# Sigmoid attention with a token-mixing MLP: 64x64 tiles, output blocks per batch, named PSUM banks and a new order of steps

## The chip, the core and the metric

The kernel runs on one core of a Trainium2 chip. A core has a matrix engine (TensorE, called PE in the profile, with its weight loads as PEld), a vector engine (DVE), a scalar engine (ACT), a general engine (POOL) and a queue engine (SP) that here only issues DMAs. Matrix products are written to PSUM, which the kernel holds as 8 banks of 128 x 512 float32, used mostly in four pairs; everything else lies in SBUF. The metric is the device time of one execution in microseconds (us). Three runs of the kernel before gave 185.79, 185.96 and 186.71 us; the median is 185.96 us.

## The reference

For 8 batches of 12 heads, with 448 tokens and 64 features per head:

```python
scores = q @ k.T / 8 - log(448)              # per batch and head
x = (sigmoid(scores) @ v)                     # heads laid side by side: (8, 448, 768)
wq, wk = x @ w_q, x @ w_k                     # (8, 448, 64) each
W_tok = wq @ wk.T / 8                         # (8, 448, 448)
out = relu(W_tok @ x) @ w_out                 # (8, 448, 768), float32
```

There is no softmax, so a sigmoid block needs nothing from its neighbours. The kernel uses (wq @ wk.T) @ x = wq @ (wk.T @ x): wk.T @ x is a 64 x 768 matrix, called `tmp`, and the 448 x 448 matrix is never made.

## The kernel before, in words

**Units.** The four heads of a batch that are worked together are a quad; 8 batches give 24 quads, three per batch. Tokens of a head lie as 7 blocks of 64. For each quad and each block there is one score step (letter `S` in the plan, function `scores`): four 64x64 matmuls of 448 columns into one pair of banks, and one sigmoid on ACT over 128 x 896 that writes a tile `at`. So there are 168 score steps and 168 sigmoids. Seven value steps (`P` or `p`, `values`) accumulate the quad's product with v in a pair of banks, and a copy to SBUF makes `xt`, which is x transposed.

**q and k** come from HBM in float32. They are cast to bfloat16, most of them on POOL, and must be transposed. There are several ways, chosen by letter: on PE with a copy out of PSUM (`q`, `k`, `a`, `b`), on DVE by its 32x32 stream transpose after POOL has exchanged quadrants (`c`, `d`; `arrange`, three pairs of POOL copies per quad), or on DVE alone with four more transposes of 32 partitions (`r`, `s`, `z`; `quadrants`).

**The MLP of a batch.** `tr_x` (`x`, `X`, `y`, `Y`) transposes `xt` to `xn`, in 64x64 tiles or whole; the token axis is padded from 448 to 512. `mlp_wqk` (`W`, `L`, `l`) makes wq and wk, in whole-array matmuls or in 64x64 tiles whose two halves are added on DVE. `mlp_wkn` (`N`) transposes wk, `mlp_tmp` or `mlp_tmp_tiled` (`U`, `T`) makes `tmp`, `mlp_mix` (`M`, `m`) multiplies it with wq and applies the ReLU on DVE or ACT into `mx`. The output product (`O`, `o`, `I`, `i`) then has three forms, for pairs of batches w = 0 to 3: `out_chunk` in whole-array matmuls over 128 tokens (w = 0 and most of w = 3), `out_pair` in 64x64 tiles (w = 1 and 2, listed in `TW`) and `out_halves` (the first half of w = 3). Results are copied to `o` tiles, or late to the idle load buffers `ld`, and stored by DMA on SP, the last ones on ACT's queue.

**Order.** `PLAN` is a string written by hand; a loop reads it letter by letter and issues the work in that order, so every engine's order is fixed by it. `ORDER` gives the order of loads and casts: six load buffers form a ring, a load is issued when the buffer's last content was cast, and `BEHIND` holds five loads back until a numbered matmul has run. `F` in the plan issues a matmul of zeros, 512 columns wide, that computes nothing; ten of the eleven such matmuls of 512 columns stand before the 20th score, and 32 smaller ones run at the very start. Pairs of banks are given out first in, first out by `bank2`; `bank1` gives half a pair.

**What limits overlap.** A score step needs a free pair. Pairs are also held by value sums (seven steps long), by output blocks, by transposes and by the MLP's products. When the pair of a score was last read by the sigmoid just before it, PE and ACT take turns.

Of the kernel before, what the change touches and what calls it, by code (L numbers as in the profile page):

```python
# [17 lines left out]
def kernel(  # L18
# [49 lines left out]
    free2 = [0, 1, 2, 3]  # L68
    halves = []

    def bank2():
        n = free2.pop(0)
        return n, pairs[n], pairs16[n]

    def bank1():
        if halves:
            n, b = halves.pop(0)
        else:
            n, b = free2.pop(0), 0
            halves.append((n, 1))  # L80
        return (n, b), pairs[n][:, b], pairs16[n][:, b]

    def release(fb):
        if isinstance(fb, int):
            free2.append(fb)
        elif (fb[0], 1 - fb[1]) in halves:
            halves.remove((fb[0], 1 - fb[1]))
            free2.append(fb[0])
        else:
            halves.append(fb)  # L90
# [5 lines left out]
    spare = singles.tile([P, 8], F32)  # L96
# [3 lines left out]
    xts = [singles.tile([P, 2, 512], BF16, name=f"xt{n}") for n in range(2 * NJ)]  # L100
    wqks = [singles.tile([P, 512], BF16, name=f"wqk{n}") for n in range(2)]
    wq2s = [singles.tile([P, S], BF16, name=f"wq2{n}") for n in range(2)]
# [25 lines left out]
    def xt(u, j):  # L128
        return xts[u % 2 * NJ + j]


    TW = (1, 2,)
# [3 lines left out]
        "FSSFFFFKSSSqFFSSkFFSSDPpSFpPSPPPqSSkPSPPSSpPpPSabSXSPpSSPSPr"  # L136
        "PXpSPSSFSszSWWWWXSPWWPSppPNSpPSqkSSUSXSMSPpSMPpSppPSSqkSPpPP"
        "SPSWWcPSPXSWWSSdMWXSWSPpPpSpNPPSqSkSUSxSMSPpppSppSCPoSOSMSOo"
        "SqCkSOoCMSpPpSDpPcPSPSdoOSSocOSLLDLSXSdLLSLPPpSppPSPSoOSoSNC"
        "xSOcDSUSPPDSPprCdPpSPpSsPpPDPSPSoPSXoSMSOoSzLLxSLLLLScSoXoSM"  # L140
        "ppDpSPpDCSpdPSOOcSpppSpPSPPSONMSYOSxSOdOSpPpPpSSDPPoOSxSUcSL"
        "LLDdSSLLLppPSppPPSoSoMSOcSOSDdPpPPSPMoPSoPmOSOScdOoSxoSDOSON"
        "oSxSOOSSUpSppPSMcpPpLLLSLpPSPdLLpDDPPSOpoSxoSOmocDSoMSodooDS"
        "NOSoSOSPPPPDtcpSppOoSMoSODoSoSdMOOSPPScpppPSOPmoOSoxoDSdOSoS"
        "OLLSLLLSLoSooNxScoPppxSpdPSPPoSODDSoSOSOOSxoSOSTppPpPSpPpPpP"
        "mPppmmWWWWWWyyINiiitiiIMiiMMIiioOoOoOOoOoOoOOOO"
    )
    PLAN = "".join(PLAN)
    KIND = ["a"] + [t for t in PLAN if t in "qacer"]
# [6 lines left out]
    def arrange(n, eng):  # L156

        arranged.add(n)
        if KIND[n] in "er":
            return  # L160
# [21 lines left out]
    def load1(n, nm, eng, m):  # L182
        u, j = quads[n]
        if KIND[n] in "cer" and nm != "v":
# [19 lines left out]
    def cast1(n, nm, e):  # L204
        if KIND[n] in "cer" and nm != "v":
# [48 lines left out]
    moves = []  # L254

    def move():
        n, m = moves.pop(0)
        for g in range(2):
            for h in range(2):
                own, other = 64 * g + 32 * h, 64 * g + 32 * (1 - h)  # L260
                nc.sync.dma_start(
                    out=qk[n][other : other + 32, h].rearrange("p t i n -> p (t i n)"), in_=m[own : own + 32, 1 - h],
                )

    def tr(n, nm, kind):
# [9 lines left out]
        if kind in "cdef":  # L275
# [5 lines left out]
            if kind in "ef":  # L281
                if t == 0:
                    moves.append((n, p_mv.tile([P, 2, 2 * S], BF16, tag="mv", name="mv")))
                nc.vector.transpose(out=moves[-1][1][:, t].bitcast(F32), in_=w)
# [5 lines left out]
        if kind in "abh":  # L290
            transposes_whole(ps[:, t], t16, slice(0, NI))
        else:
            transposes(ps[:, :, t * S : (t + 1) * S], t16, slice(0, NI))
# [9 lines left out]
        if t == 1:  # L303
            qk[n] = p_qk.tile([P, 2, 2, NI, NP], BF16, tag="qk", name="qk")
            copy = COPY["s" if kind in "jh" else "v"]
            if kind in "abh":
                copy(
                    out=qk[n].rearrange("p h t i n -> p t i h n"),
                    in_=ps[:, :, 0 : 2 * S].rearrange("p t (i h n) -> p t i h n", i=NI, h=2),
                )  # L310
            else:
                copy(
                    out=qk[n].rearrange("p h t i n -> p t h (i n)"),
                    in_=ps[:, :, 0 : 2 * S].rearrange("p h (t x) -> p t h x", t=2),
                )
# [19 lines left out]
    def values(n, i, tail, eng):  # L335
# [10 lines left out]
        if i == NI - 1:  # L346
            if tail:
                for h in range(2):
                    COPY["vs"[h]](out=xt(u, j)[:, h, 0:S], in_=ps[:, h, 0:S])  # L349
            else:  # L350
                COPY[eng](out=xt(u, j)[:, :, 0:S], in_=ps[:, :, 0:S])  # L351
# [4 lines left out]
    def tr_x(n, tail, whole, eng):  # L356
        u, j = quads[n]
        if j == 0:
            xns[u] = p_x.tile([P, 4, D], BF16, tag="xn", name="xn")
        if whole:  # L360
            fb, _, ps = bank1()
            ps = ps.rearrange("p (m g h d) -> p m g h d", m=4, g=2, h=2)
            for h in range(2):
                for m in range(4):
                    mt(
                        ps[:, m, :, h], xt(u, j)[:, h, m * P : (m + 1) * P], ident16
                    )
# [603 lines left out]
```

## Time and profile before

| what | value |
|---|---|
| median of three runs | 185.96 us |
| profiled execution, first to last instruction | 184.0 us |
| PE busy | 174.7 us (95%) |
| ACT busy | 162.7 us (88%) |
| DVE busy | 133.1 us (72%) |
| POOL busy | 124.3 us (68%) |
| moved by DMA | 48.51 MB, mean 264 GB/s |

The profiled execution's span is 184.0 us; the time of a run counts some 2 us more than that span (185.96 - 184.0 = 1.96 us against the median). Busy time on PE includes matmuls that wait in its pipeline, so a busy PE need not run at its peak; four 64x64 matmuls run side by side in the array, so their durations overlap. Rows of groups give the number of instructions, the union of their busy time, and the mean duration of one. Rows of the timeline give start, length, engine, line, operation and count of a merged group, with the idle time before it in brackets.

### The profile page before, as it was taken

The numbers are of one execution on the slowest core, as the hardware profiler recorded it, in microseconds if no ns is written. First come the engines' busy times: TensorE is split into PE (matmuls) and PEld (weight loads), VectorE is DVE, ScalarE is ACT, GpSimd is POOL, SyncE is SP. The second block draws the span as 40 slices with busy tenths as digits, with TensorE's granted clock in tenths as the row PEclk, the third lists the DMA queues.
The fourth block names the chain that finished last, engine by engine and source line by source line (L and its number), as shares of the span: only waits on it lengthen the run. The fifth ranks groups of instructions, "written<-read, shape, count | busy, mean of one in ns | idle before, by whom it ended". The sixth has DMA issues, their size and how long they took to land.

```text
span 184.0 us, 8547 instructions
## 1 busy us (share of the span) xinstructions
PE 174.7 (95%) x3662; PEld 115.3 (63%) x3662; DVE 133.1 (72%) x209; ACT 162.7 (88%) x209; POOL 124.3 (68%) x171
## 2 busy tenths in 40 slices
PE   7888989999999999999999999999999999999990
PEld 7344545554545464565555778667898878869660
DVE  3334878788798887899797788587678476686820
ACT  4699999999999999999999989999999989876230
POOL 1458799995799899779999996999999920000000
PEclk9999999999999999999999999999999999999998
DMA  5999999969999999989987984798997443422596
GB/s 177 356 385 383 328 361 360 379 229 304 331 357 326 298 289 332 344 291 315 337 298 232 349 284 145 221 321 226 352 309 226 106 125 89 116 62 60 133 237 171
DMA packets 26085, 48.51 MB, mean 264 GB/s; under 512 B 3968, under 2 KB 19968, under 8 KB 26048
## 3 DMA queue, kind: packets, MB, share of 16 engines
q1 hardware_dynamic: 25888, 47.79, 79.9%
q8 instruction: 28, 0.46, 1.1%
q10 hardware_dynamic: 160, 0.20, 0.4%
q14 instruction: 9, 0.07, 0.1%
HBM read 35.78 MB, written 11.01 MB: 254 GB/s over the span
## 4 chain that ended last, share of the span: by engine, by line
PE 78%; ACT 14%; issue 3%; DVE 2%; ACTq 0%
PE banks L119 73%; ACT at L329 13%; PE banks L122 6%; DVE xt L351 1%; DVE mx L480 1%; ACTq L661 0%; DVE ld L680 0%; DVE wqk L426 0%; ACT xt L349 0%; ACT wq L428 0%; ACT ld L678 0%; DVE zeros L716 0%; ACTq L329 0%; ACTq L678 0%; ACTq L428 0%
## 5 line engine op out<-in xcount | busy, mean ns | idle before, releaser
L329 ACT ACTIVATE at<-banks 128x896 bf16<-128x896 f32 x168 | 141.2, 932 | 4.8 <-PE banks L119 4.3
L119 PE MATMUL banks<-wout,mx 64*64 64x384 bf16 (+2 forms) x954 | 68.5, 323 | 0.0
L119 PE MATMUL banks<-qk 64*64 64x448 bf16 x672 | 61.8, 358 | 2.0 <-ACT at L329 1.3
L119 PEld LDWEIGHTS <-mx 64*64 64x64 bf16 (+1 forms) x954 | 41.1, 105 | 14.4 <-issue 5.1
L119 PE MATMUL banks<-at,v 64*64 64x448 bf16 x672 | 45.6, 351 | 0.2
L119 PEld LDWEIGHTS <-qk 64*64 64x64 bf16 x672 | 25.5, 105 | 21.4 <-issue 12.6
L209 POOL CAST qk<-ld 128x896 bf16<-128x896 f32 x28 | 33.6, 1210 | 5.4 <-DVE qk L280 1.4
L119 PEld LDWEIGHTS <-v 64*64 64x64 bf16 x672 | 22.7, 106 | 9.2 <-issue 2.4
L351 DVE CAST xt<-banks 128x896 bf16<-128x896 f32 x19 | 20.7, 1088 | 10.2 <-PE banks L119 9.8
L480 DVE TENSOR_SCALAR mx<-banks 128x1024 bf16<-128x1024 f32 (+2 forms) x21 | 21.1, 1011 | 3.9 <-PE banks L119 3.1
L219 POOL CAST v<-ld 128x896 bf16<-128x896 f32 x23 | 21.6, 954 | 1.9 <-DMA ld<-in_v_dram 1.6
L168 POOL COPY qk<-qk 32x448 uint32<-32x448 uint32 x28 | 16.4, 587 | 1.6
L280 DVE STREAM_TRANSPOSE qk<-qk 128x448 f32<-128x448 f32 x28 | 17.4, 629 | 0.0
L171 POOL COPY qk<-swap 32x448 uint32<-32x448 uint32 x28 | 15.9, 568 | 1.6
L165 POOL COPY swap<-qk 32x448 uint32<-32x448 uint32 x28 | 15.7, 562 | 1.7
L560 DVE COPY o<-banks 128x768 f32<-128x768 f32 x11 | 10.5, 952 | 5.7 <-PE banks L119 4.1
L122 PEld LDWEIGHTS <-xt 64*64 64x64 bf16 (+1 forms) x528 | 10.9, 107 | 3.6 <-issue 2.4
L119 PE MATMUL banks<-xt,wqk 64*64 64x448 bf16 (+1 forms) x138 | 12.7, 350 | 0.1
L122 PE MATMUL banks<-ident,xt 64*64 64x64 bf16 (+1 forms) x528 | 12.4, 198 | 0.1
L395 DVE COPY xn<-banks 128x1024 bf16<-128x1024 bf16 (+1 forms) x14 | 9.0, 648 | 3.3 <-PE banks L122 2.7
L119 PE MATMUL banks<-wqk,tmp 64*64 64x256 bf16 (+1 forms) x72 | 8.9, 298 | 0.1
L119 PE MATMUL banks<-wq,tmp 64*64 64x256 bf16 (+1 forms) x72 | 9.0, 300 | 0.0
(73 smaller groups left out, 159.1 us busy)
## 6 DMA issues: line engine op xcount, KB each, us to landing
ld<-in_q_dram SPq DMA_DIRECT2D x24, 448.0 KB, 5.8
ld<-in_v_dram SPq DMA_DIRECT2D x24, 448.0 KB, 5.7
ld<-in_k_dram SPq DMA_DIRECT2D x23, 448.0 KB, 6.2
out_dram<-o SPq DMA_DIRECT2D x42, 192.0 KB, 4.8
ld<-in_moe_w_out_dram SPq DMA_DIRECT2D x6, 384.0 KB, 6.2
out_dram<-ld SPq DMA_DIRECT2D x11, 192.0 KB, 2.8
wout<-wout SPq DMA_DIRECT2D x12, 96.0 KB, 6.7
out_dram<-ld SPq DMA_DIRECT2D x4, 96.0 KB, 2.4
```

Source lines behind the costliest of these rows:

```text
L119: products.append(nc.tensor.matmul(*args, **kw))
L122: products.append(nc.tensor.transpose(*args, **kw))
L165: eng.tensor_copy(out=z[lo], in_=w[hi, 0])
L168: eng.tensor_copy(out=w[hi, 0], in_=w[lo, 1])
L171: eng.tensor_copy(out=w[lo, 1], in_=z[lo])
L209: COPY[e](out=f[:, :, "qk".index(nm)].rearrange("p e i d y -> p e y i d"), in_=ld.pop((nm, n)).rearrange("p (y i e d) -> p e y i d", y=2, ...
L219: COPY[e](out=t16.rearrange("p i b d -> p b i d"), in_=ld.pop((nm, n)).rearrange("p b (i d) -> p b i d", i=NI),)
L280: nc.vector.transpose(out=qk[n][:, t].rearrange("p t i n -> p (t i n)").bitcast(F32), in_=w)
L329: nc.scalar.activation(at, sc[:, :, 0:S], ACTF.Sigmoid, bias=attn_bias, scale=attn_scale)
L351: COPY[eng](out=xt(u, j)[:, :, 0:S], in_=ps[:, :, 0:S])
L480: nc.vector.tensor_scalar(dst, ps, moe_scale, 0.0, ALU.mult, ALU.max)
L560: COPY["s" if act else "v"](out=o, in_=ps[:, :, 0:NB])
```

## The change

- **Token axis without padding.** `xt` is laid out as 7 blocks of two 64-wide halves, `xn` as 7 blocks of 64 per head pair. `tr_x` makes 28 tiled or 7 whole transposes per quad instead of 32 or 8. `mlp_wkn` makes 14 transposes instead of 8, `mlp_tmp` always runs in 64x64 tiles into a pair of banks (28 matmuls of 192 columns), with one copy out.
- **wk product.** `W` steps may be whole or tiled as before, by letter. In all there are 72 tiled and 30 whole matmuls (120 and 18 before).
- **Output blocks per batch.** `TW` becomes (1, 2, 3). An output block covers tokens of one batch, and one block per pair of batches joins the middle tokens of both. For that, wq is extended by 32 columns (`extended`), and `mlp_mix` uses 224 columns in place of 256. `out_halves` and the late case of `out_chunk` are gone; batches 0 and 1 keep the whole-array form.
- **Last store.** The last block is copied in two halves by DVE and ACT and stored in eight DMAs of 32 x 384, four on SP and four on ACT.
- **Banks by name.** `BANKS` lists for each step which pair (0 to 3) or bank (a to h) it takes.
- **Order.** `PLAN` and `ORDER` are new. The fillers `F`, the list `BEHIND`, casts by DVE and ACT (marked with a dot before), and memsets of the padding are gone. More quads are transposed by DVE alone (`r`): the program has 24 + 8 more stream transposes on DVE, fewer casts there, and 12 more q or k casts of that layout on POOL.

```diff
-    free2 = [0, 1, 2, 3]
-    halves = []
+    BANKS = (
+        "abcd01230130213201301301230130123123c20d32c032d0120210231021"
...
+    given = list("".join(BANKS))
+    held = set()
     def bank2():
-        n = free2.pop(0)
+        n = int(given.pop(0))
...
-    TW = (1, 2,)
+    TW = (1, 2, 3,)
     PLAN = (
-        "FSSFFFFKSSSqFFSSkFFSSDPpSFpPSPPPqSSkPSPPSSpPpPSabSXSPpSSPSPr"
...
-        "mPppmmWWWWWWyyINiiitiiIMiiMMIiioOoOoOOoOoOoOOOO"
+        "SSSKSSDqSDSkSPPSPSDSPPDqkSPPrSSSPspPSSpSSPDDpzPprSxSsPPPSSPp"
...
+        "SoSOpDPppSppSPoOSoSUPopPMmppPLPLlMLyLLxOyoONoOUOoMoOmOMOOoOO"
+        "ooOoOooOOOOOo"
     )
 def tr_x
-        for m in range(4):
-            for h in range(2):
+            for i in range(NI):
                 for g in range(2):
-                    for c in range(2):
+                    for h in range(2):
                         mt(
-                            ps[HALF[c], g, (2 * m + h) * HD : (2 * m + h + 1) * HD],
+                            ps[HALF[h], g, i * NP : (i + 1) * NP], xt(u, j)[HALF[g], h, i],
...
 def mlp_tmp
-        for m in range(4):
+        for i in range(NI):
             for y in range(2):
-                mm(
-                    ps[HALF[y]], wkn[u][:, m, :], xns[u][:, m, y * NB : (y + 1) * NB],
+                for x in range(2):
+                    mm(
+                        ps[HALF[x], y, 0 : NJ * DH], wkn[u][HALF[y], i, :], xns[u][HALF[y], NJ * x : NJ * x + NJ, i, :],
...
 def out_pair
+        at = S // 2 - 32 if len(us) == 2 else k * NP + (32 + S // 2 if us[0] else 0)
         for b in range(3 * part, 3 * part + 3):
-            for y, (u, i) in enumerate(blocks):
+            for y in range(2):
+                st = mx[HALF[y], b, at : at + NP]
...
+        def store_last():
             for y in range(2):
                 for x in range(2):
+                    cols = slice(x * NB, (x + 1) * NB)
+                    dma = (nc.scalar if y else nc.sync).dma_start
+                    for u in us:
+                        dma(
+                            out=out[2 * w + u].rearrange("(r n i) d -> i r n d", r=2, i=NI)[NI // 2, y, :, cols],
+                            in_=o[64 * x + 32 * u : 64 * x + 32 * u + 32, y],
+                        )
...
-    BEHIND = {("w", 1): 728, ("v", 8): 856, ("q", 22): 2264, ("v", 20): 2392, ("v", 23): 2648}
+    BEHIND = {}
```

More of the change, by code (lines that the diff above doesn't have):

```diff
@@ L289, in tr @@
         fb, _, ps = ps_qk[n]
[L290 to L293, printed above, removed]
+        transposes(ps[:, :, t * S : (t + 1) * S], t16, slice(0, NI))
         if n == 1:
@@ L396, in tr_x @@
+        if tail:
+            for g in range(2):
+                COPY["vs"[g]](out=xn[:, g], in_=ps[:, g])
+        else:
+            COPY[eng](out=xn, in_=ps)
         release(fb)
@@ L474, in mlp_tmp_tiled @@
+        COPY["s" if act else "v"](out=tmps[u], in_=ps[:, :, 0 : NJ * DH])
         release(fb)
@@ L556, in out_pair @@
         if part < 3:
-            opened.append((w, blocks, part + 1, fb, ps))
+            opened.append((w, us, k, part + 1, fb, ps))
             return
-        o = o_tile([P, 2, NB])
-        COPY["s" if act else "v"](out=o, in_=ps[:, :, 0:NB])
+        late = len(cast) == len(ORDER) + 2
+        last = w == NU // 2 - 1 and len(us) == 2
+        o = ld_next()[:, 0:D].rearrange("p (b x) -> p b x", b=2) if late else o_tile([P, 2, NB])
+        if last:
+            for y in range(2):
+                COPY["vs"[y]](out=o[:, y], in_=ps[:, y, 0:NB])
+        else:
+            COPY["s" if act else "v"](out=o, in_=ps[:, :, 0:NB])
         release(fb)
-        (u0, i0), (u1, i1) = blocks
         def store():
@@ L625, in out_halves @@
+        stores.append((o_tiles[0] - 1, store_last if last else store))
+        if tail or late:
             flush()
```

453 lines of the change are left out of this document (165 added, 288 removed), and 10 rows, old and new, of the table ORDER.

## The prediction, made before the changed kernel had run

> **What bounds the kernel now.** I read the page, then the busy time by stretch, then the timeline. From the page:
>
> ```profile
> span 184.0 us, 8547 instructions
> ...
> PE 174.7 (95%) x3662; PEld 115.3 (63%) x3662; DVE 133.1 (72%) x209; ACT 162.7 (88%) x209; POOL 124.3 (68%) x171
> ...
> PE 78%; ACT 14%; issue 3%; DVE 2%; ACTq 0%
> ```
>
> By the chain this is a PE kernel. Cut at the first sigmoid (6.29 us), the end of the last (160.99) and the last matmul (179.70), it looks otherwise (columns: length, then busy time of PE, PEld, DVE, ACT, POOL, granted clock, DMA share, GB/s):
>
> ```profile
> 6.29:51.00 44.71, 41.12 (x860) 21.91 (x857) 31.31 (x43) 44.31 (x54) 35.12 (x43) 1.00 0.98 342
> 51.00:98.00 47.00, 46.77 (x804) 26.34 (x803) 40.88 (x58) 46.59 (x60) 42.05 (x57) 1.00 0.95 315
> 98.00:161.00 63.00, 63.00 (x1630) 49.38 (x1632) 46.25 (x64) 59.38 (x73) 45.81 (x65) 1.00 0.72 222
> ...
> 179.70:184.00 4.30, 0.00 (x1) 0.00 (x0) 0.36 (x1) 0.32 (x1) 0.00 (x0) 0.80 0.59 164
> ```
>
> Up to 161 us ACT is busy in 44.31 + 46.59 + 59.38 = 150.3 of 154.7 us. PE only catches up from 98 us on, and there ACT still has 94%. So there are two limits almost at the same height, and whatever is taken from PE counts only until ACT is full. What a sigmoid costs ACT, with the first and the last of them:
>
> ```profile
> 6.29 1.73 ACT L329 ACTIVATE at<-banks 128x896 bf16<-128x896 f32 x2 [0.63 <-PE banks L119]
> ...
> 8.33 4.97 ACT L329 ACTIVATE at<-banks 128x896 bf16<-128x896 f32 x6 [0.32 <-PE banks L119]
> ...
> 98.65 9.97 ACT L329 ACTIVATE at<-banks 128x896 bf16<-128x896 f32 x12 [0.24 <-PE banks L119]
> ...
> 160.07 0.92 ACT L329 ACTIVATE at<-banks 128x896 bf16<-128x896 f32 x1 [0.68 <-PE banks L119]
> ```
>
> Twelve in 9.97 us is 0.831 us each, 139.6 us for the 168 of them. The phase of sigmoids runs from 6.29 to 160.99, 154.7 us.
>
> **The change part by part: ACT.** What else ACT does within that phase:
>
> ```profile
> L478 ACT ACTIVATE mx<-banks 128x1024 bf16<-128x1024 f32 x3 | 3.1, 1028 | 0.0
> ...
> L351 ACT CAST xt<-banks 128x896 bf16<-128x896 f32 x3 | 2.7, 912 | 0.0
> L560 ACT COPY o<-banks 128x768 f32<-128x768 f32 x3 | 2.4, 805 | 0.0
> ...
> L680 ACT COPY o<-banks 128x384 f32<-128x384 f32 x5 | 2.4, 482 | 0.1
> ...
> L370 ACT COPY xn<-banks 128x1024 bf16<-128x1024 bf16 x1 | 1.0, 1006 | 0.0
> ```
>
> That is 3.1 + 2.7 + 2.4 + 2.4 + 1.0, and one more copy of 128x384 (0.5): 12.1 us. With the sigmoids 151.7, which leaves 3.0 us of the 154.7 in which ACT has nothing or stretches. In the changed program ACT has, ahead of its last sigmoid, 6 copies of 128x384 (2.9), 5 ReLUs of 896 (as the sigmoid's 0.92: 4.6), one xn copy of 896 (at most 1.0) and a copy of 64x448 with one of 64x32 (not in these rows; between 0.5, one copy of 384, and 1.0, two; I take 0.7, since the second is small): 9.2 us. ACT is relieved of 2.9 us. If its idle 3.0 stays, the phase takes 139.6 + 9.2 + 3.0 = 151.8 us. One piece of that idle time is the 0.32 us ahead of the third sigmoid: the plan began with two scores and now issues three before the transposes `K`, so I drop it: 151.5 us, **3.2 less**.
>
> **PE** must keep that pace. What a matmul and a change of shape cost:
>
> ```profile
> 87.15 0.36 PE L119 MATMUL banks<-qk 64*64 64x448 bf16 x4
> 87.44 1.15 PE L119 MATMUL banks<-wout,mx 128*128 128x384 bf16 x6
> 88.52 0.38 PE L119 MATMUL banks<-qk 64*64 64x448 bf16 x4
> 88.73 0.74 PE L119 MATMUL banks<-at,v 64*64 64x448 bf16 x12
> 89.30 0.36 PE L119 MATMUL banks<-qk 64*64 64x448 bf16 x4
> ```
>
> From start to start, 12 tiled matmuls of 448 take 0.57 us: 448 columns at 2.4 per ns, a quarter for each, is 0.56. Six whole ones of 384 take 1.08, against 6 x 0.16 = 0.96; the four ahead of them 0.29 against 0.187. So tiled and whole work cost the same per column, and each passage between the two shapes loses 0.10 to 0.12 us. In the order of the programs there are 84 passages before and 51 after: 33 x 0.11 = 3.6 us less.
>
> Columns: of the x transposes
>
> ```profile
> L122 PE MATMUL banks<-ident,xt 64*64 64x64 bf16 x448 | 6.2, 194 | 0.0
> L122 PE MATMUL banks<-ident,xt 128*128 128x128 bf16 x80 | 6.2, 220 | 0.1
> ...
> L119 PE MATMUL banks<-zeros 128*128 128x512 bf16 x11 | 3.4, 381 | 0.3 <-ACT at L329 0.2
> ```
>
> (448 x 16 + 80 x 128) / 2400 = 7.25 us become (532 x 16 + 35 x 128) / 2400 = 5.41. By the same count, from the two programs, q and k transposes go from 3.73 us (336 tiled, 28 whole) to 1.76 (184 and 10; DVE takes the others), tmp from 4.88 (40 of 384 columns on half the array, 42 on a quarter) to 4.48 (224 of 192), the mix from 4.80 (96 of 256, 48 of 448) to 4.48 (144 of 224, 24 of 448), wk transposes from 0.85 (64 on half the array) to 1.49 (112), zeros beside the first 32 from 2.4 to 0. Scores, values, wk product and output blocks keep their columns (816 tiled and 126 + 12 whole output matmuls become 1008 and 84 of the same sum). Together 6.3 us fewer, and 9.9 with the passages; the stretch behind the last score grows by 0.5 (below), so 10.4 in the phase. PE sinks below ACT there, and PE's saving beyond 3.2 us buys nothing. The Trainium skill, TensorEngine Tiling (Array Packing), section Performance Considerations, "PSUM Bottleneck", warns that tiling speeds TensorE and not the evacuation of PSUM. If PE alone counted, the time would fall by over 10 us; by that rule it does not, and ACT's rows above agree.
>
> **DVE** gets more:
>
> ```profile
> L249 DVE STREAM_TRANSPOSE qk<-qk 32x448 f32<-32x448 f32 x8 | 5.1, 636 | 0.2
> ...
> L480 DVE TENSOR_SCALAR mx<-banks 128x1024 bf16<-128x1024 f32 x9 | 11.0, 1224 | 2.5 <-PE banks L119 1.8 <-ACT xt L351 0.6
> ...
> L312 DVE COPY qk<-banks 128x1792 bf16<-128x1792 bf16 x5 | 5.4, 1089 | 1.0 <-ACT at L329 0.6 <-PE banks L122 0.3
> ...
> L209 DVE CAST qk<-ld 128x896 bf16<-128x896 f32 x4 | 3.5, 883 | 0.0
> ```
>
> 32 more stream transposes by 0.636 are +20.4 us. Away go those 4 casts and 5 of k, v and wout (as 0.883: 7.9), 3 of 5 qk copies (3.3) and an eighth of nine ReLUs (1.2). The rest has both signs and I leave it: +8 us. In the phase DVE is busy 31.3 + 40.9 + 46.3 = 118.4 us and idle 36.3; it would be busy 126 of 151.5, idle 25. I cost this at nothing; its cover is that idle time, and what it costs without it is rival A.
>
> **POOL** gets 12 casts more and 12 exchange copies fewer:
>
> ```profile
> POOL 1458799995799899779999996999999920000000
> ...
> L209 POOL CAST qk<-ld 128x896 bf16<-128x896 f32 x28 | 33.6, 1210 | 5.4 <-DVE qk L280 1.4
> ...
> L165 POOL COPY swap<-qk 32x448 uint32<-32x448 uint32 x28 | 15.7, 562 | 1.7
> ```
>
> 12 x 1.21 - 12 x 0.56 = +7.8, less six plain q and k casts, plus three of v and wout (nearest row 1.21 each): +4. POOL's work ended in slice 33 of 40, each 4.6 us, so by 152; 4 more end by 156, ahead of the last sigmoids. That is its cover, and I cost it at nothing; uncovered, the last scores come up to 4 us late. Loads keep their bytes; dropping `BEHIND` only lets five of them start earlier.
>
> **Tail.** Behind the last score:
>
> ```profile
> 159.61 0.40 PE L119 MATMUL banks<-qk 64*64 64x448 bf16 x4
> ...
> 162.22 0.87 PEld L119 LDWEIGHTS <-wqk 128*128 128x128 bf16 x6 [0.36 <-issue]
> ...
> 163.46 0.62 PEld L122 LDWEIGHTS <-xt 64*64 64x64 bf16 x64 [0.37 <-issue]
> ...
> 179.34 0.58 ACTq L661 DMA_DIRECT2D out_dram<-ld  x1
> 180.04 0.32 ACT L678 COPY ld<-banks 128x192 f32<-128x192 f32 x1 [1.79 <-PE banks L119]
> 180.39 0.50 ACTq L661 DMA_DIRECT2D out_dram<-ld  x1
> ```
>
> PE goes from 159.61 to 179.70, 20.09 us. Columns behind the last score: 18.46 us (9 values 1.68, mixes 1.12, wk products 1.12, transposes 0.54, tmp 0.56, output 5.76 tiled and 7.68 whole) and three passages (0.33); 1.30 is waiting in the chain xt, wk product, wk transpose, tmp, mix. Afterwards 19.33 us (7 values 1.31, mixes 1.12, wk products 1.12, transposes 0.75, two tmp 1.12, 29 steps of output 13.92), no passage. Output steps now stand between all links of that chain, so I take 0.4 of waiting, from 0 to the old 1.3: 19.7 us, **0.4 less**. The end, from the last matmul to the last instruction, is 4.30 us. After the change each half of the last block is 128x384 (0.48 against 0.32), and four stores instead of one stand behind it on ACT's queue, and as many on SP's. An issue takes 0.50 to 0.58, so the last one comes 3 x 0.53 later: **1.8 more**, bounds 0 (if issues overlap) and 2.3 (if the last ones also wait 0.5 for earlier stores).
>
> **Sum** on the profiled span: 184.0 - 3.2 - 0.4 + 1.8 = 182.2; with the 1.96 us between span and median, **184.2 us**, 0.9% faster.
>
> **Rivals.** A, DVE takes ACT's place. With 32 more transposes in order before copies that free banks, a late copy holds a pair and the next score waits. If DVE needed all 36.3 us of idle time that it had, the phase would take 126.4 + 36.3 = 162.7 us, 11 over my 151.5; with half of that, 189.8 us, slower. It decides as soon as DVE needs more than 25 us. For it: from 51 to 98 us DVE is already busy 87%. Against: much of its idle time ends on PE, which now comes earlier.
>
> B, the cold clock eats the gain. The first matmuls ran at half speed:
>
> ```profile
> 0.98 3.60 PE L119 MATMUL banks<-zeros 128*128 128x128 bf16 x32 [0.98 <-DVE zeros L716]
> ```
>
> 112 ns per 128 columns, against 53 at 2.4 per ns. Without the fillers PE has 9.4 us of columns for the first 24 scores in 20 us. At half speed that is 18.9, still covered, but each score takes 0.19 longer; a third of 24 uncovered is 1.5: 185.7 us, no change. Against: granted clock 1.00 in the three stretches with sigmoids. The Trainium skill, TensorE: Matmul & The Clock Gate, Part 1, puts the drop behind an idle window of about 3.4 us; by that rule it does not happen here.
>
> C, ACT's idle time goes as well, since PE no longer holds it up and banks are named: another 3.0 us, 181.2. For it: scores whose pair was last read by the sigmoid right before fall from 8 to 3 in the programs.
>
> **How the numbers follow.** Forecast (183.2 to 185.0) 0.42, C (below) 0.20, B (to 186.9) 0.18, A 0.20. 0.5% is what a measurement here can tell from no change: faster 0.62, same 0.18, slower 0.20. The range goes from C, 181.0, over B to a third of A's full price, 187.8; the forecast's own is 183.2 to 185.0.
>
> **What would show it.** Last sigmoid's end near 157.8 (ACT step), the last score 1.4 ahead of it as before; ACT over 97% busy up to there; PE with gaps in 98 to 158; last matmul near 176.2; 6.1 us from it to the end; four stores in a row on ACT's queue. DVE as the releaser of scores would mean A; whole matmuls at 112 ns per 128 columns before 30 us B. If the phase isn't shorter at all, my main step is wrong.

## The result and the profile after

| kernel | runs | median us | lowest to highest |
|---|---|---|---|
| before | 4 | 186.05 | 185.79 to 186.71 |
| after | 4 | 190.78 | 190.10 to 191.81 |

The changed kernel is slower: ratio 1.026, with a 95% interval of 1.021 to 1.031, where 0.9% faster was forecast. Here and below, a median and a range are of all executions of a kernel, while a ratio and its interval leave out those that took over 1.5% longer than the fastest of the same kernel. From its page, the rows that answer those of before:

```profile
span 189.7 us, 8858 instructions
...
PE 170.4 (90%) x3835; PEld 118.2 (62%) x3835; DVE 139.9 (74%) x211; ACT 159.7 (84%) x201; POOL 125.0 (66%) x167
...
PEclk9966999999999999999999999999999999999998
...
PE 68%; DVE 16%; issue 5%; DMA 4%; ACT 3%; SPq 1%; POOL 0%; DVEq 0%; ACTq 0%
```

PE and ACT are both busy less than before, in a longer span: nobody took over, time went empty. The same cuts as before, by stretch (length, then busy time of PE, PEld, DVE, ACT, POOL, granted clock, DMA share, GB/s):

```profile
6.27:51.00 44.73, 37.50 (x783) 21.04 (x784) 35.10 (x53) 43.36 (x53) 36.29 (x43) 0.92 0.96 332
51.00:98.00 47.00, 44.91 (x806) 25.49 (x802) 42.31 (x63) 44.26 (x58) 39.31 (x51) 1.00 0.95 311
98.00:165.10 67.10, 64.48 (x1650) 51.79 (x1653) 49.55 (x69) 61.03 (x72) 48.04 (x67) 1.00 0.70 217
...
184.25:189.70 5.45, 0.01 (x3) 0.00 (x0) 0.56 (x1) 0.48 (x1) 0.00 (x0) 0.84 0.59 153
```

The phase of sigmoids now runs from 6.27 to 165.07, 158.8 us instead of 154.7. What ACT has to do in it (groups of that stretch):

```profile
L308 ACT ACTIVATE at<-banks 128x896 bf16<-128x896 f32 x168 | 141.4, 928 | 10.2 <-PE banks L122 7.9 <-issue 1.1
L441 ACT ACTIVATE mx<-banks 128x896 bf16<-128x896 f32 x5 | 4.6, 917 | 0.2 <-PE banks L122 0.2
L587 ACT COPY o<-banks 128x384 f32<-128x384 f32 x6 | 3.0, 498 | 0.0
L360 ACT COPY xn<-banks 128x896 bf16<-128x896 bf16 x1 | 0.9, 912 | 0.0
L407 ACT CAST wq<-banks 64x448 bf16<-64x448 f32 x1 | 0.5, 524 | 0.3 <-DVE wqk L403 0.3
L409 ACT CAST wq<-banks 64x32 bf16<-64x32 f32 x1 | 0.2, 176 | 0.0
```

Its work beside the sigmoids is 4.6 + 3.0 + 0.9 + 0.5 + 0.2 = 9.2 us, as forecast. With the 139.6 of the sigmoids that makes 148.8, and 10.0 us of the 158.8 are left as idle time, where the forecast had 2.7. Nearly all of that stands ahead of sigmoids, and PE ends it. So the question is what holds PE up.

**Place one: 98 to 125 us.** PE's timeline of the changed kernel, the rows around three of its gaps (the bracket is the idle time ahead of a row and what ended it; "issue" means that PE waited for nothing that the profile shows):

```profile
112.48 0.35 PE L122 MATMUL banks<-wout,mx 64*64 64x384 bf16 x2
113.99 0.68 PE L122 MATMUL banks<-wout,mx 64*64 64x384 bf16 x10 [1.16 <-issue]
...
117.75 1.07 PE L122 MATMUL banks<-wout,mx 64*64 64x384 bf16 x20
119.63 0.35 PE L122 MATMUL banks<-wout,mx 64*64 64x384 bf16 x2 [0.81 <-issue]
...
123.85 0.84 PE L122 MATMUL banks<-wout,mx 64*64 64x384 bf16 x14
125.01 0.68 PE L122 MATMUL banks<-wout,mx 64*64 64x384 bf16 x10 [0.32 <-issue]
```

The gaps stand in the middle of an output block, whose inputs were all there: at its third, its 23rd and its 15th matmul. No semaphore explains that. The count between them does. The two stretches from gap to gap:

```profile
113.98:119.62 5.64, 4.83 (x128) 4.19 (x128) 3.90 (x6) 4.25 (x5) 5.34 (x8) 1.00 0.96 289
119.62:125.00 5.38, 5.06 (x128) 3.97 (x128) 4.38 (x6) 4.69 (x6) 4.60 (x7) 1.00 0.96 335
```

Each holds exactly 128 matmuls and 128 weight loads: 256 instructions. The DMA side of the first of them, cut in two at 117.2 us (queue, packets, MB, share; then issues with their KB and us to landing):

```profile
q1 hardware_dynamic: 637, 1.07, 96.4%
...
ld<-in_v_dram SPq DMA_DIRECT2D x2, 448.0 KB, 6.3
```

and from 117.2 to 118.4:

```profile
q8 instruction: 1, 0.02, 4.6%
```

For 3.2 us after a block of instructions begins, the DMA engines carry only loads and stores, and the loads take 6.3 to 6.5 us from issue to landing; then comes a single packet on the queue named "instruction" (30 packets make 0.49 MB over the span, so 16 KB each, 64 bytes for each of 256 instructions). It lands at 118.08, and PE goes on at 119.62. In the trace of this kernel six blocks from 98 to 125 us and one at 172.9 start 1.30 to 1.55 us after their packet has landed, each behind a gap of 0.29 to 1.44 us; three more start as soon, without one. At all others the packet landed 1.6 us ahead or more, and no gap is over 0.11. In the kernel before only one block, at 125.5 us, starts so soon after its packet, behind a gap of 0.25.

The Trainium skill, Runtime: NRT & Kernel Launch, section Instruction fetch mechanics, says that engines refill their instruction memory in blocks of 16 KiB or 256 instructions, over a DMA queue of their own, at a cost that is "mostly hidden". The size agrees with the trace; in this kernel it is not hidden, with up to 1.44 us at one block.

**Place two: the start.** The granted clock, in the changed kernel and then in the one before:

```profile
6.27:10.49 4.22, 2.45 (x68) 1.22 (x68) 1.50 (x4) 4.22 (x6) 2.27 (x3) 1.00 1.04 384
10.49:17.32 6.83, 5.92 (x136) 3.55 (x137) 1.52 (x2) 5.60 (x7) 5.87 (x7) 0.50 1.04 393
```

```profile
6.29:10.49 4.20, 3.53 (x62) 1.44 (x59) 1.84 (x5) 3.88 (x5) 1.46 (x2) 1.00 1.04 384
10.49:17.32 6.83, 6.10 (x163) 2.96 (x155) 2.67 (x4) 6.83 (x10) 5.21 (x6) 1.00 1.05 386
```

Without fillers PE is busy 2.45 of 4.22 us, then has half the clock for 6.83 us; ACT gets 7 instructions done there instead of 10 and idles 1.23 us. Of the 3.41 us just ahead of the fall, PE is busy in half:

```profile
7.08:10.49 3.41, 1.67 (x60) 0.93 (x52) 1.21 (x3) 3.41 (x6) 1.75 (x2) 1.00 1.05 396
```

**Place three** is DVE. The table of PE's waits (total, times, longest) has it beside the block starts; the longest single one is for a bank that DVE reads late, at 69.7 us:

```profile
PE banks L122 <- issue: 2.5, 4, 1.2
...
PE banks L122 <- DVE xt L331: 1.1, 3, 0.5
PE banks L125 <- issue: 1.0, 1, 1.0
...
PE banks L125 <- DVE o L587: 0.9, 1, 0.9
```

All of PE's waits on DVE, but for the zeros at the very start, sum to 4.4 us, against 0.5 in the kernel before, and the page's chain gives DVE 16% where it gave 2%. Whether that is part of the loss is seen below, in a run that keeps these waits.

The 2.5 and the 1.0 understate the block starts: idle time counts from a matmul's modelled end, some 0.3 us late, so small gaps vanish. From the start of one matmul to the next, less the time that the first needs in the array, the gaps at 98.13, 102.96, 107.78, 113.98, 119.62 and 125.00 are 1.30, 0.38, 0.29, 1.44, 1.09 and 0.60, 5.1 us in all. "Gap" means that below.

### The profile page after: what moved, and what is told of

Its sections match the earlier page's. It is cut to its first block, busy times and chain, and to the rows that moved or that the text cites. A ratio compares the mean times of both kernels' runs of the same rounds, so it can differ in the third digit from the quotient of the medians.

```text
span 189.7 us, 8858 instructions
## 1 busy us (share of the span) xinstructions
PE 170.4 (90%) x3835; PEld 118.2 (62%) x3835; DVE 139.9 (74%) x211; ACT 159.7 (84%) x201; POOL 125.0 (66%) x167
## 4 chain that ended last, share of the span: by engine, by line
PE 68%; DVE 16%; issue 5%; DMA 4%; ACT 3%; SPq 1%; POOL 0%; DVEq 0%; ACTq 0%
PE banks L122 64%; PE banks L125 5%; DVE qk L253 4%; DMA ld<-in_k_dram 4%; DVE xt L331 3%; ACT at L308 3%; DVE mx L443 3%; DVE qk L266 2%; DVE tmp L436 1%; DVE wqk L405 1%; DVE qk L291 1%; DVE wqk L403 1%; POOL k L223 0%; DVE qk L283 0%; DVE ld L529 0%
## 5 line engine op out<-in xcount | busy, mean ns | idle before, releaser
L308 ACT ACTIVATE at<-banks 128x896 bf16<-128x896 f32 x168 | 141.4, 928 | 10.2 <-PE banks L122 7.9
L122 PE MATMUL banks<-wout,mx 64*64 64x384 bf16 (+1 forms) x1092 | 68.6, 323 | 2.5 <-issue 2.5
L122 PE MATMUL banks<-qk 64*64 64x448 bf16 x672 | 65.4, 364 | 4.5 <-ACT at L308 1.8
L213 POOL CAST qk<-ld 128x896 bf16<-128x896 f32 x40 | 46.9, 1193 | 12.7 <-DVE qk L273 4.8
L122 PE MATMUL banks<-at,v 64*64 64x448 bf16 x672 | 50.7, 360 | 1.1 <-ACT at L308 0.7
L122 PEld LDWEIGHTS <-qk 64*64 64x64 bf16 x672 | 28.8, 107 | 22.8 <-issue 15.5
L331 DVE CAST xt<-banks 128x896 bf16<-128x896 f32 x23 | 24.9, 1083 | 2.9 <-PE banks L122 2.6
L253 DVE STREAM_TRANSPOSE qk<-qk 32x448 f32<-32x448 f32 x32 | 20.4, 636 | 0.8
L443 DVE TENSOR_SCALAR mx<-banks 128x896 bf16<-128x896 f32 (+1 forms) x19 | 17.8, 939 | 3.6 <-PE banks L122 3.5
L360 DVE COPY xn<-banks 128x896 bf16<-128x896 bf16 x20 | 12.3, 615 | 5.2 <-PE banks L125 5.0
L531 DVE COPY ld<-banks 128x768 f32<-128x768 f32 x8 | 7.7, 958 | 7.8 <-PE banks L122 6.7
```

The lines of the kernel that those rows point to most:

```text
L122: products.append(nc.tensor.matmul(*args, **kw))
L213: COPY[e](out=f[:, :, "qk".index(nm)].rearrange("p e i d y -> p e y i d"), in_=ld.pop((nm, n)).rearrange("p (y i e d) -> p e y i d", y=2, ...
L253: nc.vector.transpose(out=qk[n][other : other + 32, h].rearrange("p t i n -> p (t i n)").bitcast(F32), in_=w[own : own + 32, 1 - h],)
L308: nc.scalar.activation(at, sc[:, :, 0:S], ACTF.Sigmoid, bias=attn_bias, scale=attn_scale)
L331: COPY[eng](out=xt(u, j), in_=ps)
L443: nc.vector.tensor_scalar(dst, ps, moe_scale, 0.0, ALU.mult, ALU.max)
```

## The experiments

Theory: TensorE's instruction blocks arrive late because their packet waits behind loads, and a cold clock costs some more at the start. Rivals: banks and DVE's order hold PE up; or the clock is all of it. A ratio is to the kernel before, run beside it on the same chip (its medians there were 185.6 to 186.0).

**Fillers put back.**

```diff
-        "SSSKSSDqSDSkSPPSPSDSPPDqkSPPr...
+        "FSSSFFFFKSSDqFFSDSkFFSPPSPSDSPPDqkSPPr...
+        if t == "F":
+            mm(pairs[n][:, 0], zeros[:, 0:P], zeros, start=True, stop=True)
```

> The changed kernel with nine of the dropped filler matmuls (zeros, 512 columns, into the pair that the next step takes) put back into the first steps; nothing else. Theory (cold clock): the granted clock stays at 1.0 from 8 us on, sigmoid 12 starts near 16.4 us instead of 17.67, and the time falls by about 1.3 us, to some 189.5, no more, since the later stalls at starts of instruction blocks stay (eight of them, about 5 us), only at other work, the stream being nine matmuls longer. Rival (the clock is only a bystander, the early steps are bounded by loads): sigmoid 12 stays near 17.6 us and the time within 0.5 us of the changed kernel. Rival (the cold clock is the whole cause): under 186.5.

The clock's part came true in the profile. Stretch of the start, then the waits, of this run (its profiled execution is the slowest of four, 192.87 us):

```profile
10.49:17.32 6.83, 4.94 (x118) 2.42 (x117) 2.75 (x4) 6.83 (x9) 5.69 (x6) 1.00 1.04 398
```

```profile
PE banks L122 <- issue: 5.3, 5, 2.0
```

Clock 1.00, ACT without a hole, sigmoid 12 at 16.04 us instead of 17.67. But the median is 191.33 (188.71 to 192.87), ratio 1.021 (1.012 to 1.030), which can't be told from the changed kernel's 1.026. In the profiled execution what was gained came back at block starts, where gaps were 0.95, 1.44, 1.62 and 2.26 us, four in front of matmuls 1631, 1759, 2143 and 2271. Those are numbers at which the changed kernel stalls too, though every step now stands nine matmuls later. So the clock is not the whole cause (under 186.5 us was the sign of that), and the gaps keep to a place in the stream.

**Lighter loads.**

```diff
+    def cut(n):
+        return slice(0, 2 * HD) if n >= 15 else slice(None)
...
-                out=t, in_=SRC[nm]...
+                out=t[:, cut(n)], in_=SRC[nm]...[:, cut(n)]
```

> The changed kernel in which the loads of q, k and v for the quads from 15 on move only the first 128 of 896 columns, so that about a seventh of their bytes is left; the rest of those tiles keeps old data, and the output from there on is not the reference's. All compute instructions stay. Theory (TensorE waits at starts of instruction blocks because the fetch of the block queues behind loads): the gaps of 0.3 to 1.4 us at 98 to 125 us go, ScalarE's idle time there too, and the time falls by 3 to 5 us, to 186 to 188. Rival (the gaps come from banks and from VectorE's order): the time stays within 1 us of 190.8, and the gaps are seen at the same matmuls.

185.34 us, ratio 0.999 (0.996 to 1.003): 5.4 us under the changed kernel. The stretch from 98 us, first of the changed kernel:

```profile
98.00:125.10 27.10, 24.48 (x644) 19.36 (x647) 20.79 (x29) 23.52 (x28) 23.11 (x32) 1.00 0.87 283
```

then of this run:

```profile
98.00:125.10 27.10, 26.98 (x696) 21.09 (x689) 23.49 (x33) 26.23 (x33) 25.17 (x35) 1.00 0.44 115
```

All engines have the same instructions, and in the same 27.1 us PE does 52 matmuls more. The packets now start 0.4 to 1.8 us behind the beginning of a block, where the ones for the six late blocks had started 2.4 to 4.2 behind it, and from 90 to 130 us no gap at a block start is over 0.15. Such a block lasts some 4.7 us; less 0.95 for the packet's transfer and 1.3 from its landing to the start of the next block, that leaves the packet some 2.4 us (an estimate from these rows), and the six late ones began at the edge of that or behind it. Before 98 us packets of the changed kernel began up to 3.5 us behind with no gap, since the blocks they stood in were longer. Banks and DVE's order are as they were, and PE's waits on DVE still sum to 4.2 us, at the time of the kernel before; so that rival falls as the cause of the loss. In this profile the clock stayed at 1.00 without fillers; it does not fall in every execution.

**Loads held behind the fetch, with all bytes.**

```diff
-    BEHIND = {}
+    BEHIND = {("q", 17): 1496, ("v", 16): 1624, ("k", 19): 1752, ("q", 19): 1880, ("v", 18): 2008, ("q", 21): 2136, ("q", 22): 2264}
```

> The changed kernel with seven of its loads held until a given matmul has run, seven matmuls ahead of a block's start (numbers 1496, 1624, 1752, 1880, 2008, 2136 and 2264), so that each is issued just behind the fetch of the next block instead of ahead of it. All bytes and all instructions stay. Theory (fetch behind loads): the fetches there start sooner after the block before has begun, gaps at block starts fall from about 5 us in sum to under 3, and the time falls by 2 to 4 us, to 187 to 189. Rival (loads matter only by their bytes, or the held loads come too late): no gain, or up to 2 us slower, with waits on the held tiles in place of the gaps.

187.40 us (185.60 to 191.28), ratio 1.007 (1.003 to 1.010): 3.4 us won by a list of seven numbers. From 90 to 130 us all gaps at block starts are under 0.2; one of 1.08 is left at 136.2, where no load was held, and one of 0.58 at 73.3.

**The kernel before, its loads set free.**

```diff
-    BEHIND = {("w", 1): 728, ("v", 8): 856, ("q", 22): 2264, ("v", 20): 2392, ("v", 23): 2648}
+    BEHIND = {}
```

> The kernel before with its five held loads set free; nothing else. Theory (fetch behind loads): gaps at starts of instruction blocks appear near the five places (around matmuls 735, 863, 2271, 2399, 2655), 0.3 to 1.4 us each, in all 1 to 4 us slower, 187 to 190. Rival (as the prediction had it: the loads only start earlier, at no cost): within 0.5 us of the kernel before.

187.13 us, ratio 1.007 (1.004 to 1.010): 1.6 slower by the medians beside each other (185.56). PE's timeline has what it had not had:

```profile
126.12 0.35 PE L119 MATMUL banks<-qk 64*64 64x448 bf16 x1 [0.46 <-issue]
```

a gap of 0.77 at matmul 2399, and one of 0.33 at 2527. Of the five places named one shows in this profile; the size is at the low end.

**The kernel before without fillers.** `F` issues nothing.

> The kernel before without its filler matmuls; its held loads stay at the same matmul numbers, so still just behind the starts of blocks, while the work moves by 11 matmuls against them. Theory (the fillers keep the clock): the granted clock falls below 1.0 for some us between 8 and 30 us in some executions, and the profile then has sigmoid 12 about 1 us later than 16.3; time 185.5 to 187.5. Rival (as the prediction's rival B had it, a cold clock for the whole start): 187.2 or more. Rival (no idle stretch of over 3.4 us, so no change of clock): the clock stays at 1.0 and the time within 0.5 us of the kernel before.

187.46 us, ratio 1.009 (1.007 to 1.011). Its start:

```profile
10.49:17.32 6.83, 5.55 (x117) 3.60 (x121) 2.31 (x3) 6.01 (x8) 4.33 (x6) 0.75 1.05 386
```

Half of this stretch had half the clock, ACT idles 0.8 us in it, and sigmoid 12 comes 0.6 later. The other 1 us of the 1.6 was not traced to the clock.

**Work moved by 32 matmuls.**

```diff
-    for _ in range(32):
-        mm(pairs[3][:, 0, 0:P], zeros[:, 0:P], zeros[:, 0:P], ...
+    for _ in range(64):
+        mm(pairs[3][:, 0, 0:64], zeros[:, 0:P], zeros[:, 0:64], ...
```

> The changed kernel with 64 zero matmuls of 64 columns ahead of its work in place of 32 of 128: the same columns, and the work stands 32 matmuls later in TensorE's stream. Theory (TensorE's instructions come in blocks of 128 matmuls with their weight loads): gaps without a releaser over 0.25 us from 60 us on are again in front of matmuls 95 + 128 k of the stream, and so at other work than in the changed kernel. Rival (they belong to the work): in front of the same work, at 127 + 128 k.

186.98 us in one run, and from 60 us on no gap without a releaser over 0.25 at all. So the gaps do not belong to the work, which is the same; that they keep to 95 + 128 k this run can show only once, by a gap of 0.55 at 37.6 us, at matmul 607. The clock was at 0.50 for 6.83 us here too, so what this execution lacks of the loss is the late packets: from sigmoid 96 to sigmoid 132 it took 34.5 us, the changed kernel 39.2. All loads and bytes are the changed kernel's; where they fall against the block starts is what differs.

**Both repairs:** nine fillers, and ten holds, the seven above and `("q", 23): 2392, ("v", 22): 2520, ("v", 23): 2648`.

> The changed kernel with both repairs: nine fillers put back into the first steps, and ten loads held until seven matmuls ahead of a block's start (numbers 1496 to 2648 in steps of 128). Theory (fetch and clock explain the loss, the rest of the change works as the prediction had it): the clock stays at 1.0, the gaps at block starts sum to under 1 us, the last sigmoid ends near 159, the last matmul near 177.5, and with the 5.45 us behind it the span is near 183.3; time 184.5 to 186, no slower than the kernel before. Rival (there is a third loss in the new order): 187 or more.

186.73 us (185.41 to 190.04), ratio 1.003 (1.001 to 1.006): short of the forecast. The profiled execution, the slowest of twelve at 190.04 us, still waits at block starts:

```profile
PE banks L122 <- issue: 3.0, 4, 1.2
```

The next kernel has the same program up to its last stores, and its profile has only one such gap over 0.3 (0.66): its last matmul ends at 178.05 us, against 182.83 here. So the packets are late in some executions and not in others. That the whole spread comes from it is likely, but two profiles don't show it.

**Last chunk in four stores of both batches.**

```diff
-                    for u in us:
-                        dma(out=out[2 * w + u].rearrange("(r n i) d -> i r n d", ...)[..., cols], in_=o[64 * x + 32 * u : ...])
+                    dma(out=out[2 * w : 2 * w + 2].rearrange("u (r n i) d -> i r u n d", ...)[..., cols], in_=o[HALF[x], y])
```

> The kernel with both repairs, and its last chunk stored with four transfers of both batches in place of eight of one, two on each queue. Theory (the longer end is the row of four issues on each queue): the time from the last matmul to the end falls from about 5.4 us to about 4.2, and the time by 1.0 to 1.2 us against the kernel with both repairs. Rival (the end is the transfers themselves, their bytes being the same): within 0.3 us of it.

A plain miss: 194.36 us, 7.6 more. The end of that run:

```profile
184.00:190.00 6.00, 0.00 (x0) 0.00 (x0) 0.00 (x0) 0.00 (x0) 0.00 (x0) 0.50 0.12 45
```

DMA share 0.12 is two of sixteen engines, at 45 GB/s. The merged store's outermost length is 2, the batches. The Trainium skill, DMA: Bandwidth & Descriptors, section Rules for kernel authors, says that a short outermost dimension confines a transfer to as many engines; the row agrees.

**Loads let go six matmuls behind the block's start** instead of seven ahead (ten holds at 1509 to 2661).

> The kernel with both repairs, its ten held loads set free six matmuls behind a block's start (numbers 1509 to 2661) in place of seven ahead of it. Theory (a load let go ahead of the block's start still gets ahead of the fetch whenever TensorE stalls at that start, so one stall brings the next): fetches start within 1.5 us of the block before, gaps at block starts from 90 to 140 us sum to under 1 us in every profile, and the time is 185 to 186 with a smaller spread than the 185.4 to 190.0 of the holds ahead. Rival (holds only shift the same backlog; loads now come later, and casts with them): 186.7 or more, with waits on the casts.

187.28 us (185.86 to 188.07): the spread is smaller, but the time isn't. The packet behind the block start at 99.56 us still began 3.9 us after it, and PE's timeline has

```profile
105.76 0.35 PE L122 MATMUL banks<-qk 64*64 64x448 bf16 x1 [1.22 <-issue]
```

So moving the holds behind the block's start did not cure the late packets; how much stands ahead of a packet is the next suspect.

**The last chunk of one batch, in four stores,** beside those holds.

> As the run with holds six matmuls behind, and the chunk of both batches moved ahead of the last batch's three, so that the last chunk is of one batch and goes out in four transfers of 64 partitions, two on each queue, in place of eight of 32 partitions. Theory (the end is the row of four issues per queue; the merged store was slow because its outermost length was 2, so that only two of the sixteen DMA engines moved it): from the last matmul to the end about 4.3 us instead of 5.4, and the time about 1 us under that run's, 184 to 185, faster than the kernel before. Rival (the end is set by the transfers' own latency): within 0.3 us of that run.

187.56 us, nothing won, and 6.14 us from the last matmul to the end. Of its end:

```profile
177.42 3.92 SPq L538 DMA_DIRECT2D out_dram<-ld  x4
...
180.11 0.48 ACT L529 COPY ld<-banks 128x384 f32<-128x384 f32 x1 [5.08 <-PE banks L122]
180.62 1.21 ACTq L553 DMA_DIRECT2D out_dram<-ld  x2
181.43 2.00 SPq L553 DMA_DIRECT2D out_dram<-ld  x2
```

SP's two issues come 0.8 us behind the copy, since SP still issues for the chunk before, and 2.7 us pass after the last one.

**Stores of late chunks on both queues,** beside holds seven ahead.

```diff
-                    nc.sync.dma_start(
+                    (nc.scalar if late and x else nc.sync).dma_start(
```

> Fillers, the ten holds seven matmuls ahead, the last chunk of one batch in four transfers, and of each late chunk of one batch one store on ScalarE's queue and one on SyncE's, so that SyncE's queue is free when the last chunk comes. Theory (the end is the wait of the last issue in SyncE's row): last matmul to end about 4.8 us instead of 5.5 to 6.2, and the time some 0.7 us under the 186.7 of the kernel with both repairs. Rival (the end is the transfers): 5.5 us or more, no gain.

190.81 us: the end is 5.3 us, and four holes of 1.2 to 1.5 us appear in ACT from 142 us on. At each of them a store on ACT's queue starts 0.03 us behind the end of DVE's copy and takes 0.63 to 0.74 us to issue, and the next sigmoid stands behind it.

**Loads spread two to a block,** beside those stores.

```diff
-        ("q", 17): 1496, ("v", 16): 1624, ("k", 19): 1752, ("q", 19): 1880, ("v", 18): 2008, ("q", 21): 2136,
-        ("q", 22): 2264, ("q", 23): 2392, ("v", 22): 2520, ("v", 23): 2648,
+        ("q", 17): 1496, ("k", 18): 1624, ("q", 18): 1752, ("v", 17): 1880, ("k", 20): 2008, ("q", 20): 2136,
+        ("q", 21): 2264, ("k", 21): 2392, ("k", 22): 2520, ("k", 23): 2648, ("v", 22): 2776,
```

> As the run with two queues, and the loads of quads 17 to 23 spread two to a block (eleven holds, 1496 to 2776), each some 5 us later than it could go. Theory (a fetch is late when three loads or two loads and two stores stand ahead of it): the fetches from 90 to 140 us start within 2.3 us of the block before, their gaps sum to under 1 us, the spread of the times gets small and the median falls to 184.5 to 185.5. Rival (the loads are too late for the casts): waits of TensorE on POOL's casts, and 187 or more.

192.78 us, but for another reason than the rival's. Every packet from 90 to 140 us started within 1.9 us, and no block start there has a gap; sigmoid 144 began at 135.95 us, 5.9 earlier than in the changed kernel. Then ACT's timeline:

```profile
142.43 0.93 ACT L441 ACTIVATE mx<-banks 128x896 bf16<-128x896 f32 x1
143.91 3.83 ACTq L538 DMA_DIRECT2D out_dram<-ld  x1
147.84 1.73 ACT L308 ACTIVATE at<-banks 128x896 bf16<-128x896 f32 x2 [4.49 <-DVE qk L273]
```

One store on ACT's queue took 3.83 us to issue, from 0.03 us behind DVE's copy; later ones in this run took 0.64, and why this one took so long stays open.

**The even loads without those stores.**

> Fillers and the eleven even holds of the run before, and all stores as the changed kernel has them (none on ScalarE's queue ahead of the last chunk). Theory (fetch and clock are the whole loss; the 4.49 us gap of the run before came from its stores on ScalarE's queue): no gap without a releaser over 0.25 us from 75 us on, last sigmoid ends near 158.5, last matmul near 177.5, span near 183, time 184 to 185.3, faster than the kernel before. Rival (a third loss, or loads too late for the casts): a gap near 148 us again, and 186 or more.

186.30 us (184.26 to 188.91), ratio 0.998 (0.994 to 1.002): 4.5 us under the changed kernel, level with the kernel before, and not the 184 to 185.3 expected. The profiled execution, of 185.12 us, is what the theory describes. Its span and ACT's group on the page:

```profile
span 183.3 us, 8877 instructions
...
L308 ACT ACTIVATE at<-banks 128x896 bf16<-128x896 f32 x168 | 140.9, 935 | 4.1 <-PE banks L122 2.6
```

and two of its stretches, the later part of the phase and the end:

```profile
98.00:158.95 60.95, 60.83 (x1577) 49.49 (x1570) 48.16 (x67) 58.65 (x70) 46.67 (x64) 1.00 0.75 231
...
177.73:183.30 5.57, 0.00 (x1) 0.00 (x0) 0.56 (x1) 0.48 (x1) 0.00 (x0) 0.78 0.54 148
```

ACT idles 4.1 us instead of 10.2, the last sigmoid ends at 158.94 instead of 165.07. Other executions of it are up to 3.8 us slower than that one, and there is no trace of them.

**The same without fillers.**

> The changed kernel with the eleven even holds alone, without fillers. Theory (the fillers are worth what the cold clock costs): 0.5 to 1.5 us more than the run with fillers, 185 to 186.5, and in the profile a granted clock under 1.0 between 8 and 18 us. Rival (the clock falls too seldom to matter, and nine fillers cost as much as they bring): within 0.4 us of the run with fillers.

187.37 us (185.69 to 190.36), ratio 1.008 (1.005 to 1.011), 1.1 more than with fillers: the difference is within the theory's 0.5 to 1.5, the time is above its 185 to 186.5. The profile is of 190.25 us. Its granted clock reads 1.00 through the first 30 us, but the trace holds no record of the clock ahead of 16.54 us, and the matmuls show what it was:

```profile
15.33 0.96 PE L122 MATMUL banks<-at,v 64*64 64x448 bf16 x8
...
16.91 0.55 PE L122 MATMUL banks<-at,v 64*64 64x448 bf16 x8
```

Four of these matmuls take 0.37 us from start to start up to 16.5 us and 0.19 behind it, so PE ran at half speed from its first matmul until then, as the theory had it. The first sigmoid comes 0.6 us later than with fillers, sigmoid 12 1.4 later. The rest went into block starts again, one of them at a place without holds, a gap of 1.29:

```profile
75.91 0.38 PE L122 MATMUL banks<-at,v 64*64 64x448 bf16 x2 [0.99 <-issue]
```

What half a clock costs differs from execution to execution: between 10.49 and 17.32 us ACT idled 1.23 us in the changed kernel (clock 0.50), 0.82 in the kernel before without fillers (0.75) and 0.27 with seven holds (0.75 too).

## Why the prediction was wrong

- **The step that failed.** By the prediction's own sign (the phase isn't shorter at all) its main step failed: the phase of sigmoids is 4.1 us longer, not 3.2 shorter. What it had wrong is the sentence "Loads keep their bytes; dropping `BEHIND` only lets five of them start earlier", costed at nothing. The sum had no term for the supply of TensorE's instructions. The five numbers that were dropped (728, 856, 2264, 2392, 2648) stand seven ahead of block starts, 95 + 128 k: they had kept loads behind the fetch. Freeing them cost the kernel before 1.6 us; holding seven loads the same way won the changed kernel 3.4, and lighter loads 5.4. The dropped list is not the whole of it, though: of the changed kernel's seven late blocks (1631 to 2271, and 3551) only 2271 is one that the old list covered. At the others it is loads in the new order that get ahead of the packet. The old list put back into the changed kernel was not run.
- **ACT's step** was right in its work (9.2 us forecast and measured) and wrong in its idle time: 10.0 us instead of 2.7. Without late packets, in the profile with even loads, the phase takes 158.94 - 6.92 = 152.0 us, 0.5 over the forecast 151.5. Against that profile the changed kernel loses 6.8 us in the phase. By starts of sigmoids 0, 12, 96, 132 and the end of the last, that is 1.8 up to sigmoid 12 (cold clock, though 0.7 of it is only that the fillers put off that profile's first sigmoid), 0.4 up to 96, 4.7 up to 132 (late packets) and -0.1 behind it.
- **PE's step**, "PE's saving beyond 3.2 buys nothing", needed PE to sink below ACT, with gaps in PE from 98 to 158 us as its sign. That isn't borne out even where instructions were there: with even loads PE is busy in 60.83 of 60.95 us. By columns at 2.4 per ns, the matmuls of that stretch need 57.0 of its 60.95 us, and before 59.2 of 63.0, some 94% both times. So PE had little room in this part of the phase, and late block starts were paid for nearly in full: 5.1 us of gaps, and 4.7 us lost from sigmoid 96 to 132. That PE's shorter work leaves less time per block is in the traces too: five blocks from 93.5 us on took 27.0 us before, and from 94.9 us on 23.5 us with even loads, so a packet has some 0.7 us less per block. That this makes late packets more frequent is argued, not shown.
- **Rival B** (the cold clock) happened in the profiled execution, at 0.50, though PE was never idle for 3.4 us. The prediction cited the Trainium skill, TensorE: Matmul & The Clock Gate, Part 1, for a drop behind an idle window. Its window of 3.4 us fits, as the cold stretch is 6.83 us, twice that; an idle one was not needed. B's price of 1.5 us was about right (sigmoid 12 came 1.36 later than before); it was one of two losses, not a rival outcome.
- **Rival A** (DVE in ACT's place) fell as the cause: PE's waits on DVE did grow, from 0.5 to 4.4 us, but they are 4.2 with lighter loads, at the old time. In the phase DVE is busy 127.0 us, 8.5 more, about the 8 forecast. POOL was forecast 4 more and has 0.7 more (125.0 against 124.3). **Rival C** fell with late packets, and without them ACT's idle time ahead of sigmoids was still 4.1, against 4.8 before.
- **The tail** was forecast 0.4 shorter. From the last sigmoid's end to the last matmul it is 18.7 us before, 19.2 after (with one block start at 172.9, gap 0.49) and 18.8 with even loads: nothing was won there, and the cause stays open. **The end** was forecast 6.1 and is 5.45, with eight stores in two rows; three other ways to store hardly shortened it or made it longer (5.3, 6.1 and 13 us), so the row of issues is not its only price.

The repaired kernel, then, equals the one before and does not beat it. Its profiled span of 183.3 comes out 1.1 us over the 182.2 of the sum: 0.6 for a first sigmoid that the fillers put off, 0.5 in the phase, 0.5 in the tail, less 0.5 at the end. Adding 1.96 us to get from span to time was 0.2 too much; in the runs on record a time is 1.7 to 1.8 us over its own span.

## What to carry to other kernels

When a list of holds or odd numbers in a kernel looks like tuning of loads, find what the numbers are counted against before costing their loss at nothing; here they were block starts of the instruction stream. A gap on PE that "issue" ended, amid a block whose inputs are there, and 128 matmuls from the next such gap, was a late instruction packet here: look at how many loads were issued between the block's start and its packet. And a change that takes work off the busiest engine makes each block of instructions shorter, here by 0.7 us, so its packet has less time to come. A forecast that shortens such an engine's work needs a term for that.

## What the runs showed of the hardware that was not expected

- PE's instructions come in packets of 16 KB, 128 matmuls with their weight loads, each over the DMA engines that carry the loads. The packets of the six blocks late between 98 and 125 us, at a DMA share of 0.87 to 0.96, began 2.4 to 4.2 us behind the start of the block before; at 0.44, in the same stretch, 0.4 to 1.8. A block that had to wait started 1.2 to 1.55 us after its packet had landed.
- The granted clock fell to 0.50 for 6.83 us behind a stretch in which PE was busy 1.67 of 3.41 us by the profile, and not in every execution (with lighter loads, the same matmuls, it did not). A granted clock of 1.00 can mean that there is no record: in one profile it read so while matmuls ran at half speed until 16.5 us.
- A store of 64 rows in two batches, outermost length 2, ran on two engines at 45 GB/s, and 13 us passed from the last matmul to the end.
- A store issued on ACT's queue started 0.03 us behind DVE's copy and took 0.63 to 3.83 us to issue; ACT had no compute in that time.
